# Linear-attention block and token-mixing MLP on one core: the copy of q's logits on ScalarE is issued ahead of VectorE's shift, and the weights' low parts behind the logits

## The chip, the cores and the metric

The kernel runs on one core of one Trainium2 chip. A core has a matrix engine (TensorE, "PE" in the profile, with its weight loads as "PEld"), three engines for element-wise work (VectorE "DVE", ScalarE "ACT", GpSimd "POOL"), and a sync engine ("SP") that here only issues DMA transfers. Each engine takes its own instructions in order; engines wait for each other on semaphores. Matrix products land in PSUM, a small memory of banks; everything else lives in SBUF. The metric is device time in microseconds for one execution.

## The reference, cut to what matters

`x` is 2048 tokens by 512 channels. With `H = 32` heads of `DH = 16`:

```python
qkv = layernorm(x) @ wqkv                       # q, k, v per head
pq, pk = q @ w_phi, k @ w_phi                   # logits, per head
phi_q = concat([softmax(pq), softmax(-pq)])     # and phi_k alike
kv, z = phi_k^T v, sum over tokens of phi_k
o = (phi_q @ kv) / (phi_q . z + 1e-6)
h = x + o @ wo
out = h + MLP over the token axis of layernorm(layernorm(h))   # w1: 2048 x 1792, gelu, w2: 1792 x 2048
```

Each softmax runs over the 16 features of a head. For a stable exponential the kernel subtracts the head's maximum from `pq`, and takes the head's minimum minus `pq` for the negative half.

## The kernel before

Tokens are taken in 16 tiles of 128 (`NT`). All products are in three parts (high by high, high by low, low by high, `mm3`, lines 62 to 64), so every operand is split into a rounded high part (a copy on ScalarE) and a low part (a subtraction on VectorE or GpSimd).

The work runs in three stages. Up to about 120 us, k, v and the first six tiles of q are projected. From about 120 to 265 us the attention is finished, tile by tile, in a loop of `NT + 3` iterations; its holes on TensorE are given to the first products of the MLP (`fill`). The rest is the MLP. From the last k tile to the end of the loop the order of TensorE, VectorE, ScalarE and GpSimd is that of the code (`manual_schedule`); the order of SyncE's DMA issues is set by a planner.

**q's logits** are what the change touches. TensorE projects a tile of q into a PSUM buffer `pu` (`q_mm`, two such buffers, one bank each). `logit_ops` (line 137 on) then returns three operations for VectorE: the maximum per head (`mx`, L152), the minimum (`mn`, L153), and `shift`. `shift` subtracts the maximum (L145) into one half of `eq`. For the first six tiles the other half is also made by VectorE (L150). For the ten tiles from 6 on (`pool` is true) ScalarE copies the raw logits from `pu` into that half (L147), and GpSimd later turns the copy into minimum minus logits (`negate`, L160). Then ScalarE takes the exponential of all of it (`exps`, L171).

**One iteration `it` of the loop** handles several tiles at once. TensorE runs in this order: numerators of tile it-1 (`s_num`, L543), output projection of tile it-2 into `po` (`s_wo`), transposes of tile it into the buffer `tn` (`s_tr`, L525), projection of a q tile into `pu` (`q_mm`), then fills. There is one `tn` buffer, used in turn by transposes and numerators, and one `po` buffer.

ScalarE: the moments of tile it-3, two evictions of the transposes (`pht`, L527), an exponential (L171), the copy of logits (L147), the normalised row and its split (`hn` L584, `hs` L57), high parts of streamed weights (`whi`, L604), and, next iteration, the numerators' high part (`oh`, L547).

VectorE: the list `ops`, which `turns` builds by taking alternately from two lists. The first holds `s_ol` (the numerators' low part `ol`, L552), the three logit operations and two sums of exponentials (L216); the second the six operations of a denominator (`s_den`, L451 to L457), whose result is `w`. Into this list, at position 3, go `s_h` (L568: `h`, the residual sum, reads `po`) and `flush` (L596: the low parts `wlo` of the weights that `stream` has loaded).

GpSimd: weighting by `w` (`s_pq`, L460), the product `ez` for a denominator (L442), negations (L160), and the low part of `hs` (L58). A tile's transposes need its weighting, and the `tn` buffer free, which `oh` and `ol` of the tile before decide. `oh` and `ol` also feed the output projection; `po` is free again once `h` has read it.

Just ahead of the loop (122 to 145 us) tiles 6, 7 and 8 of q go through the same operations; there VectorE also completes the sum of phi_k over tokens (`zacc`, L480), which TensorE multiplies by ones (L487), and scales the kv matrix (`kvS`, L508).

Of the kernel before, what the change touches and what calls it, by code (L numbers as in the profile page):

```python
# [11 lines left out]
AF = mybir.ActivationFunctionType  # L12
# [7 lines left out]
NT = S // P  # L20
# [13 lines left out]
def block_kernel(ctx: ExitStack, tc: tile.TileContext, x, xT, wT, phic, wo, w1, b1, w2, b2,  # L34
                 kvmask, ident_in, out):
    nc = tc.nc
# [97 lines left out]
    def signs(e):  # L134
        return e.rearrange("p g (a c h d) -> p (g a) c h d", a=2, c=2, h=2)

    def logit_ops(src, e, pool):

        v = src.rearrange("p (j h d) -> p j h d", h=2, d=DH)
        ev = signs(e)  # L140
        mx = wk.tile([P, NPR, 2], F32, name="mx")
        mn = wk.tile([P, NPR, 2], F32, name="mn")

        def shift():
            nc.vector.tensor_sub(ev[:, :, 0], v, mx.unsqueeze(3).to_broadcast([P, NPR, 2, DH]))  # L145
            if pool:
                nc.scalar.activation(ev[:, :, 1], v, AF.Copy)  # L147
                MN.append((ev, mn))
            else:
                nc.vector.tensor_sub(ev[:, :, 1], mn.unsqueeze(3).to_broadcast([P, NPR, 2, DH]), v)  # L150

        return [lambda: nc.vector.tensor_reduce(mx, v, axis=AX.X, op=ALU.max),  # L152
                lambda: nc.vector.tensor_reduce(mn, v, axis=AX.X, op=ALU.min),  # L153
                shift]

    def negate():

        if MN:
            ev, mn = MN.pop(0)
            nc.gpsimd.tensor_sub(ev[:, :, 1], mn.unsqueeze(3).to_broadcast([P, NPR, 2, DH]), ev[:, :, 1])  # L160

    def turns(*lists):

        return [ops[i] for i in range(max(map(len, lists))) for ops in lists if i < len(ops)]

    def run(*lists):
        for op in turns(*lists):
            op()
# [42 lines left out]
    def q_sum(t):  # L211

        assert t < SUMS or t - SUMS in W, "a tile's sums would go where others are still wanted"
        SQ[t] = sums[:, t % SUMS]
        e = signs(EQ[t])
        return [lambda c=c: nc.vector.reduce_sum(SQ[t][:, :, 1 - c], e[:, :, c], axis=AX.X) for c in range(2)]  # L216
# [144 lines left out]
    def q_mm():  # L361
        if q["mm"] < NT:
            PS[q["mm"]] = proj(q["mm"], wqh, wql, ps_q, "pu")
            q["mm"] += 1

    def q_logits(lag):
        n = q["logits"]
        if n < min(NT, q["mm"] - lag + NT * (q["mm"] == NT)):
            EQ[n] = big.tile([P, NG, P], F32, name="eq", tag="big")
            q["logits"] += 1  # L370
            return logit_ops(PS[n], EQ[n], n >= len(Q_AT))
        return []
# [7 lines left out]
    def q_sums(lag):  # L380
        n = q["sum"]
        if n < min(NT, q["exp"] - lag + NT * (q["exp"] == NT)):
            q["sum"] += 1
            return q_sum(n)
        return []
# [10 lines left out]
    v = 2  # L396
# [47 lines left out]
    def s_den(t):  # L444


        tz = az.tile([P, NPR, 2, 2], F32, name="tz")
        den = az.tile([P, NPR, 2], F32, name="den")
        W[t] = az.tile([P, NPR, 2, 2], F32, name="w", bufs=3)
        other = SQ[t]  # L450
        return [lambda: nc.vector.reduce_sum(tz.rearrange("p g c h -> p (g c h)"), heads(EZ[t]), axis=AX.X),  # L451
                lambda: nc.vector.scalar_tensor_tensor(tz[:, :, 0], other[:, :, 1], 1e-6, tz[:, :, 0],
                                                       op0=ALU.mult, op1=ALU.add),
                lambda: nc.vector.tensor_mul(tz, other, tz),
                lambda: nc.vector.reduce_sum(den, tz.rearrange("p g c h -> p g h c"), axis=AX.X),
                lambda: nc.vector.reciprocal(den, den),
                lambda: nc.vector.tensor_mul(W[t], other, den.unsqueeze(2).to_broadcast([P, NPR, 2, 2]))]  # L457

    def s_pq(t):
        nc.gpsimd.tensor_mul(heads(EQ[t]), heads(EQ[t]), W[t].rearrange("p g c h -> p (g c h)").unsqueeze(2).to_broadcast([P, 2 * H, DH]))  # L460

    def lead(it, mm):

        if 0 <= it + 3 < NT:
            s_ez(it + 3)
        negate()
        for _ in range(mm):
            q_mm()
        q_exp(0)
# [51 lines left out]
    def s_tr(t):  # L521
        PHT[t] = ak.tile([P, NG, P], F32, name="pht")
        ptr = ps_t.tile([P, 2, 4, P], F32, name="tn")
        for g in range(NG):
            nc.tensor.transpose(ptr[:, g // 4, g % 4, :], EQ[t][:, g, :], ident)  # L525
        for half in range(2):
            nc.scalar.activation(PHT[t][:, half * 4:half * 4 + 4, :], ptr[:, half], AF.Copy)  # L527

    def s_kv():

        pt = ps_o.tile([P, 2, P], F32, name="po")
        for b in range(2):
            nc.tensor.transpose(pt[:, b, :], kvS[:, 2 * b:2 * b + 2, :].rearrange("p n f -> p (n f)"), ident)
        nc.scalar.activation(kvB, pt, AF.Copy)

    def s_num(t):

        pn = ps_t.tile([P, 2, 4, P], F32, name="tn")[:, :, 0:2]
        for b in range(2):
            for c in range(4):  # L540
                for r in range(2):
                    rows, cols = slice(64 * r, 64 * r + 64), slice(32 * c, 32 * c + 32)
                    nc.tensor.matmul(pn[cols, r, b, :], kvB[rows, b, cols], PHT[t][rows, 4 * b + c, :],  # L543
                                     start=True, stop=True, skip_group_check=True)
        oh = ak.tile([P, 2, 2, P], F32R, name="oh")
        ol = ak.tile([P, 2, 2, P], F32R, name="ol")
        nc.scalar.activation(oh, pn, AF.Copy)  # L547
        OS[t] = oh, ol, pn

    def s_ol(t):  # L550
        oh, ol, pn = OS[t]
        return [lambda: nc.vector.tensor_sub(ol, pn, oh)]  # L552

    def s_wo(t):
        oh, ol, _ = OS.pop(t)
        PO[t] = po = ps_o.tile([P, D], F32, name="po")
        for j in range(4):
            mm3(po, oh[:, j // 2, j % 2, :], ol[:, j // 2, j % 2, :], woh[:, j, :], wol[:, j, :], j == 0, j == 3)

    def s_x(t):  # L560
        HT[t] = ak.tile([P, D], F32, name="h", bufs=4)
        nc.sync.dma_start(HT[t], x[t * P:(t + 1) * P, :])

    def s_h(t):

        h = HT[t]
        VE[t] = ak.tile([P, 4], F32, name="ve2", bufs=3)
        nc.vector.scalar_tensor_tensor(h, PO.pop(t), 1.0, h, op0=ALU.mult, op1=ALU.add, accum_out=VE[t][:, 2:3])  # L568
        nc.sync.dma_start(out[t * P:(t + 1) * P, :], h)

    def s_moments(t):

        junk = ak.tile([P, D], F32, name="hj", bufs=1)
        nc.scalar.activation(VE[t][:, 1:2], VE[t][:, 2:3], AF.Copy, scale=-1.0 / D)
        nc.scalar.activation(junk, HT[t], AF.Square, bias=VE[t][:, 1:2], accum_out=VE[t][:, 3:4])
        nc.scalar.activation(VE[t][:, 0:1], VE[t][:, 3:4], AF.Identity, scale=(1.0 + EPS) / D, bias=eps2)

    def s_rstd(t):
        nc.gpsimd.tensor_tensor(r2[:, t:t + 1], VE[t][:, 0:1], mhalf[:, :1], op=ALU.pow)
        nc.gpsimd.tensor_mul(VE[t][:, 1:2], VE[t][:, 1:2], r2[:, t:t + 1])  # L580
# [49 lines left out]
    for it in range(NT + 3):  # L630
        if 0 <= it < NT:
            s_x(it)
        if 0 <= it - 1 < NT:
            s_num(it - 1)
        if 0 <= it - 3 < NT:
            s_moments(it - 3)
        if 0 <= it - 2 < NT:
            s_wo(it - 2)
        if it == 1:
            run(q_logits(0))  # L640
            q_mm()
        if 0 <= it < NT:
            s_tr(it)
        if it == 0:
            s_kv()
        if 0 <= it + 1 < NT:
            s_pq(it + 1)
        if 0 <= it - 3 < NT:
            s_rstd(it - 3)
        lead(it, 1)  # L650
        den = s_den(it + 2) if it + 2 < NT else []
        ops = turns((s_ol(it - 1) if 0 <= it - 1 < NT else []) + q_logits(1) + (q_sums(0) if it > 0 else []), den)

        ops[3:3] = ([lambda: s_h(it - 2)] if 0 <= it - 2 < NT else []) + [flush]
        run(ops)
        if it > 0:
            negate()
        if 0 <= it - 3 < NT:
            s_hn(it - 3)
        if FN[0] <= it - LAG:  # L660
            fill(0, ps_f)
        for _ in range(2):
            if q["logits"] == NT and FN[1] <= it - LAG:
                fill(1, ps_q)
        for p in range(2):
            if it >= LAG - 2 and FL[p] <= FN[p] + 1:
                fill_load(p)
# [199 lines left out]
```

## Time and profile before

| | |
|---|---|
| median of 3 runs | 535.25 us (534.66 to 535.86) |
| profiled execution: time, span | 535.27 us, 533.5 us |
| mean granted TensorE clock | 0.999 |
| HBM traffic over the span | 103 GB/s |

Busy time by stretch, in us of the span (from the table of windows):

| stretch | length | PE | DVE | ACT | POOL |
|---|---|---|---|---|---|
| 0 to 40 | 40 | 38.06 | 33.16 | 35.03 | 21.25 |
| 80 to 120 | 40 | 40.00 | 35.40 | 15.27 | 34.23 |
| 120 to 130 | 10 | 9.55 | 8.46 | 7.18 | 6.78 |
| 130 to 140 | 10 | 10.00 | 9.66 | 2.44 | 9.19 |
| 140 to 150 | 10 | 10.00 | 6.50 | 4.77 | 7.06 |
| 150 to 160 | 10 | 10.00 | 9.33 | 4.46 | 9.00 |
| 160 to 170 | 10 | 10.00 | 8.86 | 6.93 | 7.10 |
| 170 to 180 | 10 | 8.63 | 8.77 | 7.90 | 8.10 |
| 180 to 190 | 10 | 9.26 | 6.81 | 6.95 | 9.83 |
| 190 to 200 | 10 | 9.83 | 8.45 | 7.58 | 7.30 |
| 260 to 533 | 273 | 268.09 | 173.72 | 110.40 | 27.50 |

How to read it: a span is the time from the first to the last instruction that the profiler saw; the device time holds a little more at both ends. Times within the trace count from the span's start. A row of a timeline gives the start, the duration, the engine, the source line and the operation with the tile it writes and those it reads; in square brackets stands how long the engine was idle just before, and whose completion ended that. Rows of one engine may overlap by some 0.1 us where instructions follow each other in a pipeline. The view of waits adds these idle times up: total, how often, longest. The ten copies of line 147 start at 126.40, 136.17, 140.71, 147.31, 150.14, 154.86, 161.48, 170.85, 177.81 and 185.90 us; the transposes of tiles 0 to 6 at 143.70, 151.18, 158.33, 165.48, 174.16, 182.72 and 192.28 us.

### The profile page before, as it was taken

The numbers are of one execution on the slowest core, as the hardware profiler recorded it, in microseconds if no ns is written. First come the engines' busy times: TensorE is split into PE (matmuls) and PEld (weight loads), VectorE is DVE, ScalarE is ACT, GpSimd is POOL, SyncE is SP. The second block draws the span as 40 slices with busy tenths as digits, with TensorE's granted clock in tenths as the row PEclk, the third lists the DMA queues.
The fourth block names the chain that finished last, engine by engine and source line by source line (L and its number), as shares of the span: only waits on it lengthen the run. The fifth ranks groups of instructions, "written<-read, shape, count | busy, mean of one in ns | idle before, by whom it ended". The sixth has DMA issues, their size and how long they took to land.

```text
span 533.5 us, 9887 instructions
## 1 busy us (share of the span) xinstructions
PE 523.4 (98%) x3872; PEld 451.0 (85%) x3872; DVE 382.5 (72%) x680; ACT 277.6 (52%) x470; POOL 228.3 (43%) x180
## 2 busy tenths in 40 slices
PE   8999999999999899999999999999999999999995
PEld 7888888887877777778788888888899999999995
DVE  6893999878798979784235523835768878887784
ACT  6998833525447777666766423525443343343340
POOL 2589699877876978985345000000001101100110
PEclk9999999999999999999999999999999999999999
DMA  8544310022302223333355333533014556535631
GB/s 303 196 124 119 86 35 21 1 62 78 101 1 83 95 81 119 120 109 111 95 159 182 99 100 99 159 111 87 20 41 110 138 149 146 131 120 120 158 78 43
DMA packets 45487, 55.85 MB, mean 105 GB/s; under 512 B 3968, under 2 KB 33024, under 8 KB 45440
## 3 DMA queue, kind: packets, MB, share of 16 engines
q1 hardware_dynamic: 43136, 51.38, 30.3%
q0 software_dynamic: 2016, 3.67, 5.1%
q8 instruction: 30, 0.49, 0.4%
q10 hardware_dynamic: 288, 0.17, 0.1%
q14 instruction: 17, 0.14, 0.1%
HBM read 46.81 MB, written 8.39 MB: 103 GB/s over the span
## 4 chain that ended last, share of the span: by engine, by line
PE 90%; DVE 5%; ACT 3%; issue 1%; POOL 1%; DVEq 0%; ACTq 0%; POOLq 0%
PE py L761 26%; PE pu L62 12%; PE pu L64 12%; PE pu L63 11%; PE po L62 3%; PE pv L63 2%; PE tn L525 2%; PE pv L64 2%; PE pv L62 2%; PE pk_ps L62 2%; PE po L63 2%; PE po L64 2%; PE pk_ps L64 2%; PE pk_ps L63 2%; PE tn L543 2%; PE kvp L207 1%
## 5 line engine op out<-in xcount | busy, mean ns | idle before, releaser
L799 POOL DMA_DIRECT2D out<-ot x14 | 12.5, 1001 | 212.1 <-DVE ot L797 212.1
L761 PE MATMUL py<-uf,whi 128*128 128x256 f32 x560 | 96.2, 283 | 0.0
L62 PE MATMUL pu<-hs,whi 128*128 128x512 f32 x224 | 87.6, 394 | 0.7 <-ACT eq L147 0.7
L57 ACT ACTIVATE whi<-wraw 128x1792 fp32r<-128x1792 f32 x28 | 47.7, 1705 | 77.9 <-PE py L761 62.9
L63 PE MATMUL pu<-hs,whi 128*128 128x512 f32 x224 | 87.2, 389 | 0.0
L64 PE MATMUL pu<-hs,wlo 128*128 128x512 f32 x224 | 87.0, 390 | 0.2 <-DVE wlo L596 0.2
L761 PEld LDWEIGHTS py<-uf,whi 128*128 128x128 f32 x560 | 83.3, 192 | 0.0
L596 DVE TENSOR_TENSOR wlo<-wraw,whi 128x512 fp32r<-128x512 f32 x56 | 46.3, 841 | 45.2 <-ACT whi L604 44.0
L761 PE MATMUL py<-uf,wlo 128*128 128x256 f32 x280 | 69.9, 283 | 0.0
L58 DVE TENSOR_TENSOR wlo<-wraw,whi 128x1792 fp32r<-128x1792 f32 x28 | 56.6, 2023 | 17.8 <-ACT whi L57 17.8
L604 ACT ACTIVATE whi<-wraw 128x512 fp32r<-128x512 f32 x56 | 34.4, 627 | 45.6 <-PE pu L63 41.6
L62 PEld LDWEIGHTS pu<-hs,whi 128*128 128x128 f32 x224 | 42.1, 188 | 9.3 <-ACT eq L147 1.2
L64 PEld LDWEIGHTS pu<-hs,wlo 128*128 128x128 f32 x224 | 42.1, 188 | 9.3 <-DVE wlo L596 0.6
L761 PEld LDWEIGHTS py<-uf,wlo 128*128 128x128 f32 x280 | 49.7, 192 | 0.0
L63 PEld LDWEIGHTS pu<-hs,whi 128*128 128x128 f32 x224 | 42.1, 188 | 8.4
L442 POOL TENSOR_TENSOR ez<-eq,zB 128x1024 f32<-128x1024 f32 x16 | 39.5, 2474 | 0.1
L761 PE MATMUL py<-un,whi 128*128 128x256 f32 x224 | 38.4, 283 | 0.0
L195 POOL TENSOR_TENSOR pk<-pk,sk 128x1024 f32<-128x1024 f32 x16 | 31.1, 1944 | 9.8 <-DVE sk L194 9.0
L460 POOL TENSOR_TENSOR eq<-eq,w 128x1024 f32<-128x1024 f32 x16 | 31.0, 1940 | 5.9 <-DVE w L457 5.9
L527 ACT ACTIVATE pht<-tn 128x512 f32<-128x512 f32 x32 | 17.4, 596 | 30.8 <-PE tn L525 30.8
L761 PEld LDWEIGHTS py<-un,whi 128*128 128x128 f32 x224 | 33.2, 192 | 0.1
L199 POOL TENSOR_TENSOR zacc<-zacc,pk 128x1024 f32<-128x1024 f32 x13 | 31.3, 2406 | 0.6
(165 smaller groups left out, 1192.8 us busy)
## 6 DMA issues: line engine op xcount, KB each, us to landing
wraw<-in_w SPq DMA_DIRECT2D x112, 256.0 KB, 2.9
xraw<-in_xT SPq DMA_DIRECT2D x16, 256.0 KB, 3.1
xh<-in_x SPq DMA_DIRECT2D x16, 256.0 KB, 2.6
h<-in_x SPq DMA_DIRECT2D x16, 256.0 KB, 3.1
out<-h SPq DMA_DIRECT2D x16, 256.0 KB, 2.0
out<-ot POOLq DMA_DIRECT2D x14, 256.0 KB, 4.6
wraw<-in_wT SPq DMA_DIRECT2D x12, 256.0 KB, 5.0
wo<-in_wo SPq DMA_DIRECT2D x4, 256.0 KB, 4.7
```

The source lines that it names most:

```text
L57: nc.scalar.activation(hi, src, AF.Copy)
L58: lo_engine.tensor_sub(lo, src, hi)
L62: nc.tensor.matmul(o, ah, bh, start=first, stop=False)
L63: nc.tensor.matmul(o, ah, bl, start=False, stop=False)
L64: nc.tensor.matmul(o, al, bh, start=False, stop=last)
L195: nc.gpsimd.tensor_mul(heads(PK[t]), heads(PK[t]), sk.unsqueeze(2).to_broadcast([P, 2 * H, DH]))
L199: nc.gpsimd.tensor_add(zacc, zacc, PK[t])
L442: nc.gpsimd.tensor_mul(EZ[t], EQ[t], zB)
L460: nc.gpsimd.tensor_mul(heads(EQ[t]), heads(EQ[t]), W[t].rearrange("p g c h -> p (g c h)").unsqueeze(2).to_broadcast([P, 2 * H, DH]))
L596: LO.append(nc.vector.tensor_sub(wl_, raw, wh_).ins)
L604: nc.scalar.activation(wh_, raw, AF.Copy)
L761: nc.tensor.matmul(o, a[x], b[:, y], start=start and i == 0, stop=stop and i == 2, skip_group_check=True)
```

## The change

```diff
@@ -140,11 +140,12 @@
         ev = signs(e)
         mx = wk.tile([P, NPR, 2], F32, name="mx")
         mn = wk.tile([P, NPR, 2], F32, name="mn")
+        if pool:
+            nc.scalar.activation(ev[:, :, 1], v, AF.Copy)
 
         def shift():
             nc.vector.tensor_sub(ev[:, :, 0], v, mx.unsqueeze(3).to_broadcast([P, NPR, 2, DH]))
             if pool:
-                nc.scalar.activation(ev[:, :, 1], v, AF.Copy)
                 MN.append((ev, mn))
             else:
                 nc.vector.tensor_sub(ev[:, :, 1], mn.unsqueeze(3).to_broadcast([P, NPR, 2, DH]), v)
@@ -649,9 +650,12 @@
-        ops = turns((s_ol(it - 1) if 0 <= it - 1 < NT else []) + q_logits(1) + (q_sums(0) if it > 0 else []), den)
-
-        ops[3:3] = ([lambda: s_h(it - 2)] if 0 <= it - 2 < NT else []) + [flush]
+        ql = q_logits(1)
+        ops = turns((s_ol(it - 1) if 0 <= it - 1 < NT else []) + ql + (q_sums(0) if it > 0 else []), den)
+
+        at = 7 if ql else 3
+        ops[at:at] = [flush]
+        ops[3:3] = [lambda: s_h(it - 2)] if 0 <= it - 2 < NT else []
         run(ops)
```

`logit_ops` now issues ScalarE's copy when it is called, so the copy of a tile stands in the program ahead of the maximum, the minimum and the shift of that tile. On ScalarE itself the sequence of instructions stays as it was. In the loop, iterations that have logits (`ql` is not empty: iterations 0 to 5) get the `flush` at position 7 of the list, which is behind the shift, and not at position 3, between the maximum and the minimum. `s_h` stays at position 3. Where the list has fewer than three operations (from iteration 14 on), `flush` now stands ahead of `s_h`; before it stood behind. Line numbers of the code behind line 143 move up by one or by four.

## The prediction

> **What bounds the kernel now.** I read the busy shares first, then TensorE's waits, then the timelines of VectorE and ScalarE around the moved instructions.
>
> ```profile
> PE 523.4 (98%) x3872; PEld 451.0 (85%) x3872; DVE 382.5 (72%) x680; ACT 277.6 (52%) x470; POOL 228.3 (43%) x180
> ```
> ```profile
> PE tn L525 <- POOL hs L58: 1.4, 1, 1.4
> ...
> PE pu L62 <- ACT eq L147: 0.7, 1, 0.7
> PE pk_ps L487 <- DVE zacc L480: 0.5, 1, 0.5
> PE pu L64 <- DVE wlo L596: 0.2, 1, 0.2
> ```
>
> TensorE (PE) is busy 98% of the span, and its order is written by hand, so a hole in it is not filled by other matmuls: it ends up in the time. In the stretch that the change touches (122 to 195 us) PE loses only these four: 2.8 us. The 1.4 us stands before the transposes of tile 4 (174.16). They also need VectorE's `ol` (L552, 173.33 plus 0.69), which clears their PSUM buffer and is itself late because ScalarE was late. The order of ScalarE and VectorE there:
>
> ```profile
> 122.83 0.63 DVE L152 TENSOR_REDUCE mx<-pu 128x32 f32<-128x512 f32 x1
> 123.37 0.68 DVE L153 TENSOR_REDUCE mn<-pu 128x32 f32<-128x512 f32 x1
> 123.96 0.68 DVE L145 TENSOR_TENSOR eq<-pu,mx 128x512 f32<-128x512 f32 x1
> 125.05 1.29 DVE L480 TENSOR_TENSOR zacc<-zacc,pk 128x512 f32<-128x512 f32 x2 [0.41 <-POOL pk L195]
> ...
> 158.02 0.68 DVE L152 TENSOR_REDUCE mx<-pu 128x32 f32<-128x512 f32 x1
> ...
> 160.05 0.68 DVE L145 TENSOR_TENSOR eq<-pu,mx 128x512 f32<-128x512 f32 x1
> ...
> 162.30 0.22 DVE L457 TENSOR_TENSOR w<-smq,den 128x64 f32<-128x64 f32 x1
> 163.63 0.69 DVE L552 TENSOR_TENSOR ol<-tn,oh 128x512 fp32r<-128x512 f32 x1 [1.11 <-ACT oh L547]
> ```
> ```profile
> 125.81 0.69 ACT L186 ACTIVATE vs<-pv,r 128x512 f32<-128x512 f32 x1 [2.16 <-PE pv L64]
> 126.40 0.59 ACT L147 ACTIVATE eq<-pu 128x512 f32<-128x512 f32 x1
> ...
> 159.46 1.09 ACT L527 ACTIVATE pht<-tn 128x512 f32<-128x512 f32 x2 [3.21 <-PE tn L525]
> 160.43 1.15 ACT L171 ACTIVATE eq<-eq,r 128x1024 f32<-128x1024 f32 x1
> 161.48 0.59 ACT L147 ACTIVATE eq<-pu 128x512 f32<-128x512 f32 x1
> 170.85 0.60 ACT L147 ACTIVATE eq<-pu 128x512 f32<-128x512 f32 x1 [2.17 <-DVE eq L145]
> ```
>
> The reader is to see two things. VectorE takes the maximum of a tile of logits well before ScalarE reaches its copy: 3.6 us earlier for tile 6 (122.83 against 126.40), 3.5 us for tile 12. And no copy begins before the shift has ended (170.14 plus 0.68, copy at 170.85): the two never read one `pu` buffer together.
>
> **The change, part by part.** Nothing is added or removed: ten copies of 0.60 us keep their place in ScalarE's order, and in the two programs' streams PE, ACT and POOL run the same sequence. What moves is the wait. In the changed stream none of the ten copies waits for VectorE any more, and all ten maxima (L152 before) wait for ScalarE, which none did. So VectorE, which ran ahead, now stands at each maximum until ScalarE has worked through what is queued before the copy. Behind the waiting maximum on VectorE are the minimum, the shift, `h`, the denominators down to `w`, and `ol`. PE waits for `ol`, `h` and, through GpSimd's weighting (L460), `w`.
>
> *Tile 6.* The copy stays at 126.40, behind `vs`, which waits for PE's `pv`; it ends at 126.99. The maximum goes from 122.83 to 127.03. From maximum to the shift's end is 124.64 - 122.83 = 1.81, so the first `zacc` sum starts at 128.84, not 125.05. PE's L487 waits for it (0.5 us already): PE loses **3.8**, and ScalarE and GpSimd, which follow PE, move along.
>
> *Tiles 7 and 8.* Here the later maximum falls into VectorE's 3.40 us of idle time before L508; nothing. Without that cover it would be 2.4 (tile 8: copy 140.71 + 3.8, so the maximum moves 6.2 against PE's 3.8).
>
> *Tile 9.* Its copy follows an exponential (146.07, next slot 147.12, plus 3.8 = 150.9), ends at 151.5, and the maximum moves from 144.18 to 151.55, by 7.4. The shift ends at 154.65; PE's projection into the same buffer (148.32) begins near 154.8. `ol` (150.02) ends at 158.1, so the transposes of tile 1 (151.18) start at 158.2: PE **+7.0** in all.
>
> *The loop, iterations 1 to 5.* From now on each iteration is a ring. Transposes to `pht` 159.46 - 158.33 = 1.13; `pht` to copy 161.48 - 159.46 = 2.02; copy to maximum 0.62; maximum to the slot of the next `ol` 162.44 - 158.02 = 4.42; `ol` 0.69 and 0.14 to the transposes (174.02 to 174.16). That is 9.02 us, where PE's own period is 165.48 - 158.33 = 7.15.
> - Iteration 1: 0.61 shorter on VectorE (no `h`: 155.56 - 151.75 = 3.81), but the exponential waits for GpSimd's negation, moved 7.4 with `w` (153.80 to 161.17). Copy 162.2, maximum 162.86, `ol` 166.67, transposes 167.5 against 158.33: **+9.2**.
> - Iteration 2: 9.02 against 7.15: **+11.0**.
> - Iteration 3: the two low parts (L596) now stand behind the shift. They hold nothing up there in ScalarE, but they are inside the ring, before `w` and `ol`. They took 169.31 - 166.57 = 2.74 beside GpSimd's L442; a pair undisturbed takes 1.29 (215.22). Here they lie beside GpSimd's negation and `hs`, so I take 2.3: 11.32 against 174.16 - 165.48 = 8.68, **+13.7** (ends 12.6 and 14.1).
> - Iteration 4: 9.02 against 8.56: **+14.1**.
> - Iteration 5: PE's fill into tile 15's buffer waited 0.74 for the copy at 185.90, 3.83 after the transposes. Now it waits for the shift: 3.18 to the copy, 0.63 to the maximum, 2.71 to the shift's end, 0.05 = 6.57. **+16.9**.
> - Iteration 6 has no logits; the 0.2 before L64 goes away: **+16.7**.
>
> From there the engines run as before, 16.7 us later, PE full, and nothing pays it back: PE's idle time after 260 us is 4.9 us of 273.
>
> *Low parts elsewhere.* Where an iteration has no logits the low parts keep their place, but from iteration 14 on, with only `ol` in the list, they come ahead of `h`. There VectorE waits 1.61 us for PE's `po`, and a pair takes 1.29: nothing, and up to 1.3 each if that idle time were gone. SyncE's order is changed in some places (stores of `out` against loads of weights); its loads wait for low parts. An issue there takes 0.3 to 0.5 us, weights are loaded an iteration ahead: nothing, at most 0.5 for each of the few swaps.
>
> *Sum:* 535.27 (span 533.5 and 1.8 around it; the median of three is 535.25) + 16.7 = **552.0**.
>
> The Trainium skill's PSUM — Partial Sum Buffer (section "PSUM bank collisions raise a hardware error") says that two engines must not touch the same PSUM bank at once, two reads included. By that rule the change can only swap who reads first; the rows above (170.82, then 170.85) agree.
>
> **Rivals.**
> 1. *The copy runs free beside VectorE* and only the waits on it go: 1.4 + 0.7 + 0.2 less, 533.0. For it: ScalarE stood 5.7 us in four waits for the shift, and that holds the 174.16 transposes up. Against: the maximum's new wait in the stream. **0.03**.
> 2. *VectorE's idle time takes it up in the loop.* It has 0.64 to 2.57 us before each `ol`, and might be let in sooner if ScalarE, freed of the shift, gets to its copies earlier than I have it. Then only tile 6 and tile 9 cost: 7.0, 542.3. Against: a copy sits behind `pht`, which PE's transposes release, and those precede it by 3.15 us whatever VectorE does. **0.08**.
> 3. *GpSimd becomes part of the ring in every iteration* as in iteration 1: negation late, exponential late, 0.9 more in each of four iterations, 555.6. For it: 3.29 us of waiting there for the copy before 171.52. Against: from iteration 3 on the exponential is of a tile negated an iteration earlier. **0.08**.
> 4. *Same as before*: the two effects cancel, 535.3. It would take 16.7 us of cover. **0.01**.
>
> My forecast has **0.80**. It is the bounds of the low parts (1.5), of the hand-overs (0.03 to 0.19 us on ten rings, about 1.5) and of the swaps on SyncE; with rival 3 above and some way towards rival 2 below, the range is 545.5 to 556.5. By the cases, slower by over 0.2% (1.1 us, about what a measurement of this kernel can tell) 0.96, within 0.01, faster 0.03.
>
> **What would show it.** The waits of the profile after should have VectorE's maximum waiting for ScalarE's copy some 20 to 30 us in total, PE waiting for `zacc` about 4.3 us instead of 0.5, and PE's transposes some 1.5 to 3 us in each of iterations 1 to 4; PE's busy time stays near 523 while the span grows. The stretch 120 to 200 becomes about 137 to 217 at its end; after 220 every event is shifted by one constant. It is wrong if the maximum starts before its copy has ended, or if the first `zacc` sum still starts near 125.

## The result, and the profile after

The changed kernel takes 557.79 us (median of five runs, 556.55 to 558.46) against 535.10 for the kernel before in the same comparison (534.66 to 535.86): a ratio of 1.0421, 95% interval 1.0404 to 1.0438. It is slower, as forecast, but by 22.7 us and not by 16.7; 557.8 lies 1.3 us above the top of the range. The profiled execution has a span of 556.0 us (before: 533.5), so the span grew by 22.5.

The page's busy line of the changed kernel, and its row of the granted clock in 40 slices of 13.9 us each:

```profile
PE 529.4 (95%) x3872; PEld 453.8 (82%) x3872; DVE 380.4 (68%) x680; ACT 276.8 (50%) x470; POOL 227.9 (41%) x180
PEclk9999999997999899999999999999999999999999
```

The counts of instructions are the same as before. PE's busy time is not: it rose by 6.0 us, from 523.4, though the same 3872 matmuls ran. And two slices have a clock below full speed (7 and 8 tenths); before, all 40 showed a 9. So the time went to two places: PE stands more, and it works longer.

**The waits.** The view of waits of the changed kernel, first over all engines, then of PE alone (total, number, longest):

```profile
DVE mx L153 <- ACT eq L144: 28.7, 9, 4.1
```
```profile
PE tn L526 <- DVE ol L553: 6.9, 4, 3.6
PE pu L62 <- DVE eq L147: 5.9, 2, 3.4
PE pk_ps L488 <- DVE zacc L481: 4.8, 1, 4.8
PE po L62 <- DVE h L569: 1.4, 2, 0.7
```

VectorE's maximum now waits for ScalarE's copy (in nine places by this view, 28.7 us), and everything that stands behind it on VectorE holds PE: `ol`, the shift (`eq` L147), the `zacc` sums, `h`. Exactly these four names were absent or small before. The timelines of VectorE and of ScalarE in the changed kernel, around tile 6 and in iteration 3:

```profile
126.71 0.69 DVE L153 TENSOR_REDUCE mx<-pu 128x32 f32<-128x512 f32 x1 [4.12 <-ACT eq L144]
127.32 0.68 DVE L154 TENSOR_REDUCE mn<-pu 128x32 f32<-128x512 f32 x1
127.92 0.68 DVE L147 TENSOR_TENSOR eq<-pu,mx 128x512 f32<-128x512 f32 x1
128.51 1.83 DVE L481 TENSOR_TENSOR zacc<-zacc,pk 128x512 f32<-128x512 f32 x2
...
183.27 0.69 DVE L153 TENSOR_REDUCE mx<-pu 128x32 f32<-128x512 f32 x1 [2.77 <-ACT eq L144]
...
185.92 2.82 DVE L597 TENSOR_TENSOR wlo<-wraw,whi 128x512 fp32r<-128x512 f32 x2
...
190.45 0.68 DVE L553 TENSOR_TENSOR ol<-tn,oh 128x512 fp32r<-128x512 f32 x1
```
```profile
126.09 0.59 ACT L144 ACTIVATE eq<-pu 128x512 f32<-128x512 f32 x1
...
180.62 1.09 ACT L528 ACTIVATE pht<-tn 128x512 f32<-128x512 f32 x2 [3.60 <-PE tn L526]
181.60 1.15 ACT L172 ACTIVATE eq<-eq,r 128x1024 f32<-128x1024 f32 x1
182.64 0.60 ACT L144 ACTIVATE eq<-pu 128x512 f32<-128x512 f32 x1
```

This is the ring of the prediction: the copy (182.64) sits behind the exponential and `pht`, `pht` waits for PE's transposes; the maximum starts 0.03 us after the copy has ended (183.24, 183.27), and `ol` comes another 7.2 us later, the pair of low parts within them. PE's next transposes need that `ol`.

**The clock.** PE's timeline of the changed kernel where the two long holes end, with rows of the projections behind the first:

```profile
129.89 3.75 PE L488 MATMUL pk_ps<-zacc,ones 128*128 128x512 f32 x4 [4.76 <-DVE zacc L481]
...
133.87 0.63 PE L63 MATMUL pu<-wql,xs 128*128 128x512 f32 x1
134.29 0.63 PE L64 MATMUL pu<-wqh,xs 128*128 128x512 f32 x1
...
136.27 0.40 PE L64 MATMUL pu<-wqh,xs 128*128 128x512 f32 x1
136.51 0.39 PE L62 MATMUL pu<-wqh,xs 128*128 128x512 f32 x1
...
191.28 1.94 PE L526 MATMUL tn<-ident,eq 128*128 128x128 f32 x8 [3.63 <-DVE ol L553]
```

and the windows of 2 us over the same place (after the length: busy time and count of PE, PEld, DVE, ACT and POOL; then the granted clock, the DMA share and GB/s):

```profile
126.00:128.00 2.00, 0.00 (x0) 0.00 (x0) 1.29 (x3) 0.68 (x2) 0.00 (x0) 1.00 0.01 4
128.00:130.00 2.00, 0.11 (x1) 0.14 (x1) 2.00 (x3) 0.00 (x0) 1.05 (x1) 0.69 0.00 0
130.00:132.00 2.00, 2.00 (x3) 0.97 (x4) 2.00 (x4) 0.03 (x1) 0.00 (x0) 0.50 0.00 0
132.00:134.00 2.00, 2.00 (x4) 0.87 (x4) 0.75 (x2) 0.89 (x2) 0.00 (x0) 0.50 0.00 0
136.00:138.00 2.00, 2.00 (x10) 1.61 (x10) 1.22 (x1) 0.00 (x0) 2.00 (x2) 1.00 0.00 0
```

The clock column falls to 0.50 while PE still stands, and stays there for the first 5.7 us of its work (129.89 to 135.6). A matmul of 128x512 is shown with 0.63 instead of 0.39 us, and the starts are 0.42 to 0.43 us apart instead of 0.23. The four ones matmuls (3.75; before 1.95) and the twelve projections behind them take 137.20 - 129.89 = 7.31 us, before 4.55: **2.76** lost. Behind the second hole the transposes and the projections take 191.28 to 197.63 = 6.35, before 174.16 to 177.82 = 3.66: **2.69**. Together 5.45 us in which PE counts as busy. In this profile the other holes (2.53 at 157.68, 3.39 at 209.04) left the clock at 1.00.

**The account.** PE's holes after: 4.76 + 2.53 + 0.48 + 1.90 + 0.72 + 0.89 + 0.69 + 3.63 + 3.39 + 0.15 = 19.14; before 2.73: +16.4. With the 5.45 of the clock that is 21.9 of 22.5. Of the other 0.6, most is PE's busy time too (6.0 against 5.45), in rows too small to name.

### The profile page after: what moved, and what is told of

It is laid out like the page before. It is cut to its first block, busy times and chain, and to the rows that moved or that the text cites. A ratio compares the mean times of both kernels' runs of the same rounds, so it can differ in the third digit from the quotient of the medians.

```text
span 556.0 us, 9893 instructions
## 1 busy us (share of the span) xinstructions
PE 529.4 (95%) x3872; PEld 453.8 (82%) x3872; DVE 380.4 (68%) x680; ACT 276.8 (50%) x470; POOL 227.9 (41%) x180
## 4 chain that ended last, share of the span: by engine, by line
PE 87%; DVE 7%; ACT 3%; issue 1%; POOL 1%; DMA 1%; DVEq 0%; POOLq 0%; ACTq 0%
PE py L765 25%; PE pu L62 11%; PE pu L64 11%; PE pu L63 11%; PE pv L63 3%; PE pv L64 3%; PE pv L62 3%; PE tn L526 3%; PE po L62 2%; PE pk_ps L62 2%; PE pk_ps L64 2%; PE pk_ps L63 2%; PE po L63 2%; PE po L64 2%; PE kvp L208 2%; PE tn L544 1%
## 5 line engine op out<-in xcount | busy, mean ns | idle before, releaser
L528 ACT ACTIVATE pht<-tn 128x512 f32<-128x512 f32 x32 | 17.4, 596 | 45.6 <-PE tn L526 45.6
```

## The experiments

All were timed beside the kernel before on the same chips (534.83 to 534.97). Where a kernel has matmuls that nothing reads, or additional sums on VectorE, they are on top of the full computation; the sums write a tile that is overwritten later. The questions were: which part of the change costs; whether the price of tile 6 is right; whether the slow matmuls behind holes are real time, and how it depends on the hole; and whether the copy can be issued early without the ring.

### The two parts alone

*Low parts only* takes the second hunk of the change alone (`at = 7 if ql else 3`); *copy only* takes the first hunk alone.

> Only the low parts go behind the logits; the copy stays behind the shift. Ring theory (the loss comes from VectorE's maximum waiting for ScalarE's copy): no loss here; the shift of tile 13 is no longer behind 2.74 us of low parts, so the hole of 1.4 us before the transposes of tile 4 shrinks: 533.6 to 534.9. Rival (the low parts, now ahead of w and ol, are what costs): 540 or more.

> Only the copy goes ahead of the maximum; the low parts stay at position 3. Ring theory: the low parts lie inside the ring in either place, so all of the loss stays: 555 to 559. Rival (low parts behind the logits cost most of it): 537 to 543.

Low parts only: 533.34 us, ratio 0.9973 (0.9962 to 0.9984), faster than before, and a little more so than I expected. Copy only: 555.31, ratio 1.0388 (1.0373 to 1.0403). PE's waits with the low parts moved alone:

```profile
PE pu L62 <- ACT eq L147: 0.6, 1, 0.6
PE pk_ps L487 <- DVE zacc L480: 0.5, 1, 0.5
PE pu L64 <- DVE wlo L596: 0.2, 1, 0.2
```

The 1.4 us before the transposes of tile 4 is gone: the low parts no longer stand ahead of the shift, so the copy and the ScalarE work behind it come earlier. All the loss is the copy's. The parts do not add up: -1.5 and +20.5 give 19.0, together they cost 22.7. With the copy ahead the low parts' new place lengthens the ring instead; PE's holes are 17.1 us in copy only, 19.1 with both, and most of the difference is the wait before the transposes of tile 4 (2.10 against 3.63).

### Tile 6 put back

```diff
-        if pool:
+        ahead = pool and q["logits"] > len(Q_AT) + 1
+        if ahead:
             nc.scalar.activation(ev[:, :, 1], v, AF.Copy)
...
             if pool:
+                if not ahead:
+                    nc.scalar.activation(ev[:, :, 1], v, AF.Copy)
```

In the changed kernel, the copy of tile 6 alone goes back behind the shift.

> The changed kernel with tile 6 alone put back (its copy behind the shift). If the losses add place by place, the hole before the zacc product and its slow clock go (4.3 + 2.8 us off TensorE's path): about 550.5. Rival (the loop's rings absorb it: they start later in the changed kernel only because tile 6 was late, and the time of the loop is set by something further back): 555 or more.

550.43 us, ratio 1.0284 (1.0269 to 1.0299): 7.4 less than the changed kernel. PE's wait for `zacc` is 0.45 again. In the changed kernel that place held 4.3 us of hole and 2.8 of slow clock, 7.1 in all, but that the time falls by as much is in part luck. In this profile the other holes are 1.1 us shorter as well (13.8 in all, after 19.1), and the clock falls at three places in the loop and not at one, behind holes of 2.52, 3.64 and 3.41 us.

### The clock measured by itself

The kernel before, with n reductions of about 1.2 us on VectorE ahead of the `zacc` sums, so that PE gets one hole at a chosen place and nothing else of the change is there; and n = 3 with 16 matmuls in that hole:

```diff
     run(q_logits(0))
+    for _ in range(n):
+        nc.vector.reduce_sum(kvS[:, 0, :], heads(PK[NT - 1]), axis=AX.X)
```
```diff
+    keep = ps_k.tile([P, D], F32, name="pk_ps", tag="pk_ps")
+    for _ in range(16):
+        nc.tensor.matmul(keep, X[NT - 1][:, 0, 0, :], wqh[:, 0, :], start=True, stop=True)
```

> One extra sum ahead of the zacc sums in the kernel before: a hole of some 2 us. Clock theory: the clock stays at 1.0, the time rises by the hole's growth alone, 1.3 to 1.8, to 536.3 to 536.8. Rival (any hole costs the slow clock): 538.5 or more.

> The kernel before with two extra sums of 1.2 us on VectorE ahead of the zacc sums: TensorE's hole there is 0.45 + 2.3 = some 2.8 us. Clock theory: this is mostly too short for the clock to drop, the time rises by about the hole, 2.3 to 2.6, to 537.2 to 537.6, perhaps up to 3 more in some executions. Rival (VectorE's delay is made good later): under 536.

> Three extra sums: a hole of some 4.0 us. Clock theory: the clock halves behind the hole for about 5.5 us, and the time rises by 3.6 + 2.8 = 6.4 to about 541.3. Rival (no clock, only the wait): 538.5.

> The three extra sums again, with 16 matmuls (3.6 us) in the hole that they make. Clock theory: the clock stays at 1.0 and only the wait of 3.65 us is left: 538.4 to 538.9, against 541.2 without the matmuls. Rival (what follows the hole is slow for another reason): 541.

| kernel | hole, us | lowest clock behind it | time, us | ratio (95%) | over 534.93 | hole's growth from 0.45 | left |
|---|---|---|---|---|---|---|---|
| n = 1 | 1.59 | 1.00 | 535.98 | 1.0019 (1.0011 to 1.0028) | 1.05 | 1.14 | -0.1 |
| n = 2 | 3.38 | 0.50 | 539.97 | 1.0089 (1.0076 to 1.0102) | 5.04 | 2.93 | 2.1 |
| n = 3 | 4.10 | 0.50 | 541.19 | 1.0111 (1.0098 to 1.0124) | 6.26 | 3.65 | 2.6 |
| n = 3, hole filled | 0.45 | 1.00 | 538.64 | 1.0063 (1.0049 to 1.0077) | 3.71 | 3.65, as filled | 0.1 |

The expectation for n = 2 missed: the hole came out 0.6 us longer than I had worked out, and the clock fell. The last two rows differ only in that PE works in the hole. The windows of n = 3, then of n = 3 with the hole filled:

```profile
126.00:128.00 2.00, 0.00 (x0) 0.00 (x0) 1.94 (x2) 0.69 (x2) 1.06 (x1) 1.00 0.01 4
130.00:132.00 2.00, 2.00 (x4) 0.73 (x3) 2.00 (x4) 0.60 (x1) 0.00 (x0) 0.50 0.00 0
```
```profile
126.00:128.00 2.00, 2.00 (x11) 1.65 (x10) 1.94 (x2) 0.72 (x2) 1.06 (x1) 1.00 0.02 4
130.00:132.00 2.00, 2.00 (x8) 1.17 (x8) 2.00 (x4) 1.35 (x3) 0.08 (x1) 1.00 0.00 0
```

The useful work waits for the same `zacc` sum (its ones matmuls start at 129.24 and 129.25), yet with the hole filled the kernel is 541.19 - 538.64 = **2.55** us faster. That is by the medians. The profile of n = 3 is of its fastest execution (540.30; the other three took 541.13 to 541.40), and there the ones matmuls and the twelve projections take 6.19 us, only 1.64 more than before. So one long hole costs its length and some 1.6 to 2.8 us again; the last section shows why there are two sizes.

### The changed kernel with its holes filled

The changed kernel with matmuls that nothing reads: 18 in the hole before the ones matmuls (one); 13 more ahead of the transposes of tile 4 (two); 10 and 13 more ahead of q's projection 11 and of the fill of iteration 5 (four).

```diff
+    for _ in range(18):
+        nc.tensor.matmul(keep, X[NT - 1][:, 0, 0, :], wqh[:, 0, :], start=True, stop=True)
     for g in range(2):
```

> The changed kernel plus 18 matmuls of 128x512 that nothing reads, put on TensorE where it waits 4.76 us for the zacc sum (18 x 0.227 = 4.1 us). Theory (a hole of over 3.4 us also drops TensorE's clock to half for some 5.5 us): clock stays 1.0 from 125 to 140 us, the second hole before the transposes of tile 4 keeps its own, and the time falls by 2.8 to about 555. Rival (the matmuls behind the hole are slow because of the other engines' traffic, not because of the hole): they stay slow, 557 to 558.5 as before or more.

> The changed kernel with matmuls that nothing reads in two of TensorE's holes: 18 ahead of the zacc product, 13 (2.95 us) ahead of the transposes of tile 4. Clock theory: what the waits alone cost is left, about 552.3 (535 plus 16.4 us of holes plus some 0.6), up to 555 in executions in which the clock drops at a third hole, which has no free PSUM buffer to be filled from. Rival (the slow matmuls are not due to the holes): 555 or more, as with one hole filled.

> The changed kernel with matmuls that nothing reads in all four of its large holes: before the ones matmuls of iteration 1, ahead of q projection 11, before the transposes of tile 4 and before the fill of iteration 5. If the slow matmuls behind the holes are the clock's answer to an idle TensorE, the granted clock stays at 1.0 throughout and the time is the waits alone: 535.1 + 16.4 + 0.5 to 1.3 of restarts = 552.0 to 552.8. If the clock drops for another reason (with one or two holes filled it only fell at another hole), it falls again somewhere and the time stays at 555 or more.

One hole filled: 555.09, ratio 1.0370 (1.0355 to 1.0384), as expected: the first slow stretch is gone, 2.70 us with it. But its profile, of the slowest of five executions (553.65 to 556.81), has a new slow stretch behind the 3.39 us hole, so the size is in part luck. Two: 555.42, ratio 1.0373 (1.0357 to 1.0389), no less than with one, and not near 552.3. In its profile the filled places stay at 1.00, but now the clock falls behind the 2.52 and the 3.39 us holes, which had left it alone in the profile of the changed kernel. That left it open whether the missing time was the clock's alone. Four: **552.52** (552.46 to 553.21), ratio 1.0328 (1.0314 to 1.0343). Its clock row and PE's waits:

```profile
PEclk9999999999999999999999999999999999999999
```
```profile
PE tn L529 <- DVE ol L556: 4.3, 5, 1.9
PE po L62 <- DVE h L572: 1.4, 2, 0.7
...
PE pk_ps L491 <- DVE zacc L481: 0.7, 1, 0.7
PE pu L62 <- DVE eq L147: 0.4, 1, 0.4
```

The useful work waits as in the changed kernel, PE merely no longer stands in the four large holes, and the time is 5.27 us less than 557.79. This is what the prediction's sum had left out, and 552.52 is 0.5 us above what it gave (552.0).

### The copy early, without the ring

Here the copies of tiles 11 to 15 are issued ahead of `pht`, when the projection is there, and not behind the exponential; tiles 6 to 10 keep the order of before. One kernel also moves the low parts, the other does not.

```diff
+        ql = q_logits(0, True) if it > 0 else []
         if 0 <= it < NT:
...
-        ops = turns((s_ol(it - 1) if 0 <= it - 1 < NT else []) + q_logits(1) + (q_sums(0) if it > 0 else []), den)
+        ql = ql if it > 0 else q_logits(1)
+        ops = turns((s_ol(it - 1) if 0 <= it - 1 < NT else []) + ql + (q_sums(0) if it > 0 else []), den)
```

> Low parts behind the logits, and in iterations 1 to 5 the copy is issued still earlier, ahead of the evictions of the transposes, where its projection is already done; tiles 6 to 10 keep the old order (copy behind the shift). Ring theory: VectorE's maximum finds the copy done or waits some 0.2 us, no ring forms, and the holes of 1.4 and 0.7 us close: 532.8 to 534.3. Rival (any copy ahead of the maximum costs, because VectorE is held by it): 540 or more.

> The copy ahead of the evictions of the transposes in iterations 1 to 5, as in the experiment before, with the low parts back at position 3. Ring theory: ScalarE is no longer held by the shift of tile 13, so hn, hs and oh come 2 us earlier and the two holes of 1.4 and 0.7 us shrink without the other edit: 532.6 to 533.8. Rival (only the low parts' move gained, the early copy does nothing): 534.5 to 535.2.

With the low parts moved: **532.37** us, ratio 0.9953 (0.9940 to 0.9965), faster than both kernels. Its ScalarE timeline and PE's waits:

```profile
155.86 0.59 ACT L145 ACTIVATE eq<-pu 128x512 f32<-128x512 f32 x1
159.17 1.09 ACT L531 ACTIVATE pht<-tn 128x512 f32<-128x512 f32 x2 [2.72 <-PE tn L529]
```
```profile
PE pk_ps L491 <- DVE zacc L484: 0.5, 1, 0.5
PE pu L64 <- DVE wlo L600: 0.2, 1, 0.2
```

The copy now lies in time in which ScalarE waited for PE's transposes, and the maximum that waits for it is not held by them: in the stretch of the change PE is left with 0.7 us of waits. The low parts' move alone had given 533.34; the two intervals overlap a little, so the gain of the early copy itself, about 1 us, rests on the waits more than on the times.

Without the low parts' move it was a miss: 536.74, ratio 1.0028 (1.0019 to 1.0036), 2.9 us above the upper end that I expected. From its profile, a low part on VectorE and what GpSimd did at the time:

```profile
181.94 2.78 DVE L600 TENSOR_TENSOR wlo<-wraw,whi 128x512 fp32r<-128x512 f32 x1
```
```profile
181.77 2.41 POOL L446 TENSOR_TENSOR ez<-eq,zB 128x1024 f32<-128x1024 f32 x1
```

The single low part took 2.78 us (0.69 in the kernel before) beside GpSimd's `ez`, in front of the shift of tile 15, and PE's fill waits 2.1 us for that shift. That undoes the gain. It does not account for the time: the profiled execution took 534.91, eleven others 535.22 to 537.47, most near 536.8. What the others had that this one had not is not traced. Eight of the eleven have a mean granted clock of 0.994, against 0.998 here and 0.992 to 0.994 with the slow stretch of n = 3, so a fall of the clock behind that hole would fit; it is not shown.

## Why the prediction came out as it did

The direction, the mechanism and nearly every wait were right. What failed is the last step, the *Sum*, "535.27 ... + 16.7", which took each hole of PE at its length and nothing for the speed of PE behind it; its other form is the sentence "PE's busy time stays near 523". The 16.7 is 16.4 in the trace. The shift of the transposes shows where the rest came in (measured: their start after less their start before, plus 0.31, by which this trace runs ahead until the first hole):

| transposes of tile | 0 | 1 | 2 | 3 | 4 | 5 | 6 |
|---|---|---|---|---|---|---|---|
| start, us | 150.47 | 161.20 | 170.46 | 179.52 | 191.28 | 202.54 | 214.78 |
| shift predicted | 3.8 | 7.0 | 9.2 | 11.0 | 13.7 | 14.1 | 16.9 |
| shift measured | 7.1 | 10.3 | 12.4 | 14.4 | 17.4 | 20.1 | 22.8 |
| difference | 3.3 | 3.3 | 3.2 | 3.4 | 3.7 | 6.0 | 5.9 |

The difference is not spread over the loop. It comes in two steps, each behind one of the two holes after which the clock fell: 3.3 at once, and 2.3 between tiles 4 and 5.

- *Tile 6.* The first `zacc` sum was put at 128.84; it started at 128.51 plus 0.31 = 128.82. The two sums took 1.83 instead of 1.29, beside GpSimd's negation, so the hole grew by 4.31 and not 3.79. With the 2.76 of the clock that is the 3.3.
- *Tiles 7 and 8* cost nothing, *tile 9* 3.25 us more than tile 6 (predicted 3.2).
- *The ring* in iterations 1 to 3: steps of 2.1, 1.9 and 3.1, predicted 2.2, 1.8 and 2.7. The low parts in iteration 3 held VectorE for 2.74 (185.92 to 188.66), where I took 2.3 between bounds of 1.29 and 2.74: 0.4 too little, at the upper bound.
- *Iteration 4* was put at 0.4; the shift grew by 2.7 there, all of it the clock's 2.69.
- *The fill of iteration 5* waits 3.39 for the shift, after a copy late by the ring; with the transposes of tile 6 it gives 2.7, predicted 2.8.
- *The rivals.* The copy does not run free: the maximum waits for it. VectorE's idle time does not take the loop up: the holes from the transposes of tile 2 on are 11.4 us. GpSimd joins the ring once, in iteration 1 (ScalarE's exponential at 164.14 stood 0.75 us for the negation), and not in the later iterations, where the exponential follows `pht` at once; 555.6, the time of that rival, is nearer to 557.8 than my own, but for another reason.
- *The range* took in the bounds of waits only. No term of it could have held the clock, and the trace of before could not show one: its longest hole in the stretch is 1.4 us.

The fall of the clock behind holes of 4.76 and 3.63 us is in the rows above. The Trainium skill, TensorE: Matmul & The Clock Gate, "Part 1: The HAM clock gate (the "warmup" mystery)", says that the array runs at half its clock once it has been idle for a window of about 3.4 us, and at the full one after about 3.4 us of work, the windows running freely. The 5.7 us of slow work would fit, since the windows need not begin with the work, and so does the slow pitch: 0.427 us by the Trainium skill, 0.42 to 0.43 here. The prediction had a hole of 4.3 us in it ("PE waiting for `zacc` about 4.3 us") and did not ask what such a hole does. By the rows the two that made the clock fall cost 2.76 and 2.69 us beyond their length.

## What to carry to other kernels

Where two engines read the same tile one after the other, the one that comes first in the program makes the other wait; put first the one that gets there first, or issue the late one's read ahead of what holds it up, as the kernel of 532.37 us does. When a change gives TensorE a hole, price the hole by its length and reckon with work at half clock behind it as well: 1.6 to 2.8 us each here, hidden in PE's busy time and shown by its clock. The shortest hole that paid this here was 2.52 us, and whether one of 2.5 to 3.4 us pays it depends on when it comes (next section). A filled hole separates the two prices, but fill all of them, since the clock may then fall behind another.

## What was not expected of the hardware

The holes that make the clock fall are not fixed by length alone. All of 3.6 us and more did (4.76, 4.10, 3.97, and 3.63 to 3.64 in three kernels), none of 2.10 and less. Between them it varied from kernel to kernel for the same hole: the 3.39 to 3.41 us before the fill left the clock alone in the changed kernel and lowered it in three others; the 2.5 us before projection 11 lowered it in three kernels and not in two. It may also fall after the work has begun again. In the profile with one hole filled, the hole before the fill ended at 206.59, and these windows follow:

```profile
208.00:210.00 2.00, 2.00 (x29) 1.21 (x35) 1.34 (x4) 0.00 (x0) 1.27 (x2) 0.52 0.47 131
210.00:212.00 2.00, 2.00 (x29) 1.35 (x14) 0.67 (x2) 1.27 (x3) 1.38 (x1) 0.63 0.00 0
```

What decides can be read from the traces. A window that holds both speeds dates the change: 0.69 over 128 to 130, shown above, is 1.24 us at half clock, so the clock fell at 128.76. In the same way these windows of the changed kernel give a rise near 135.6, a fall at 190.2 and a rise near 197.0:

```profile
134.00:136.00 2.00, 2.00 (x7) 1.57 (x6) 0.00 (x0) 1.31 (x2) 1.65 (x1) 0.60 0.00 0
190.00:192.00 2.00, 0.72 (x4) 0.76 (x5) 1.97 (x4) 0.00 (x0) 1.39 (x1) 0.55 0.39 126
196.00:198.00 2.00, 2.00 (x8) 1.63 (x7) 2.00 (x7) 1.72 (x3) 0.00 (x0) 0.74 0.09 32
```

With windows of 1 us the four times are 128.76, 135.58, 190.20 and 197.02: the falls are 61.44 us apart, 18 steps of 3.413, and each slow stretch is 6.82 us long, 2 such steps. The same grid holds in all seven profiles in which the clock falls during the work: every fall and rise within the span lies a whole number of these steps from the first, to 0.02 us. All fourteen profiles can be cut into these steps from 5 us on; where the clock falls only behind the last work, they are counted back from there. TensorE stood 1.91 us or more in each of the 14 steps ahead of a fall within the work, and 1.86 us or less in every other step at full clock. So the place of a hole in the grid decides, and not its length alone. The hole before the fill was split into 1.62 and 1.77 us in the changed kernel; with one hole filled, 1.92 of it came into one step, at whose end, at 208.08, the clock fell.

The length of a slow stretch follows the grid too. After a slow step in which TensorE stood for 0.12 us at most, the clock rose (14 of 14); after one in which it still stood for 1.07 us or more, a second slow step came (4 of 4, both falls of the changed kernel among them). That is the cost of about 1.6 us for one step and 2.7 for two.

Filling one hole moves all later ones in time, which is how the kernel with two holes filled gained nothing over that with one. The Trainium skill's page TensorE: Matmul & The Clock Gate ("Part 1: The HAM clock gate (the "warmup" mystery)") has freely running windows of about 3.4 us, and these traces agree with them. The 3.4 us that the Trainium skill gives (TensorE: Matmul & The Clock Gate, "Part 1: The HAM clock gate (the "warmup" mystery)") is not a lower bound on the hole in these runs: 2.52 us were enough in some.
